# First weight tile of an attention and feed-forward kernel loaded later and converted in halves, second-pass inputs reordered, first products of the last stage moved forward

## The chip, the cores and the metric

The kernel runs on one core of a Trainium2 chip. Its time is the device time in microseconds (us) of one execution. A core has a matrix engine (TensorE, PE in the profile, its weight loads PEld), a vector engine (VectorE, DVE), a scalar engine (ScalarE, ACT), a general engine (GpSimd, POOL) and a queue that issues transfers (SyncE, SP). Each of them works through its own list of instructions in order and waits for the others by semaphores.

## What is computed

Eight batches of eight heads, 576 positions, head size 64: masked softmax attention, then for each of the 4608 tokens a feed-forward layer of 512 to 2048 to 512 with a sigmoid gate.

```python
scores = scale * np.matmul(q, k.transpose(0, 1, 3, 2))
# heads 0 to 3: 0 <= i - j < 32; heads 4 to 7: j <= i and i % 32 == j % 32
scores = np.where(masks[None], scores, -1e9)
attn = np.exp(scores - np.max(scores, axis=-1, keepdims=True))
attn = attn / (np.sum(attn, axis=-1, keepdims=True) + 1e-09)
x = np.matmul(attn, v).transpose(0, 2, 1, 3).reshape(B * S, H * D)
h = x @ w_in
g = h * (1.0 / (1.0 + np.exp(-1.702 * h)))
out = g @ w_out
```

## The kernel before

**Numbers.** Every matmul of the feed-forward layer is made of three, since each factor is held as a high and a low part: `x_high`, `w_high`, `t_high` round a tile to its high part on ACT, and `x_low`, `w_low_part`, `t_low` subtract that from the tile on DVE. A weight tile of w_in arrives as 64-bit words (1024 KB) and is turned into float32 in three steps, `w_scale` and `w_low` on ACT and `w_join` on DVE; `w_high` then makes the high part and stores the joined words to memory (`plains`) for later. The store stands behind the copy in program order, on SP.

**Stages.** The attention is cut into 48 pairs, six for each batch. A pair goes through `scores` (PE), `masked` (DVE), `exps` (ACT), `totals` (DVE), `scaled` (POOL), `turn` (four transposes on PE and a copy on ACT), `values` (PE) and its moves (copies on ACT, or on ACT and DVE when shared). The feed-forward layer's first half, per batch, follows its six pairs. For batch 0 (the first pass) it is done plainly: `plain(n, u)`, eight units of six matmuls for each of eight weight tiles n. From batch 1 on (the second pass and later) it is done by the seven products of a Strassen scheme, `product(n, k)` with `combine(n, k)`, on the sums of x parts (`x_sum`) and of weight parts (`t_sum` on POOL). The hidden values go to memory (`hid`). The second stage, `products(n)` for 72 pieces n, reads them back (`load_g`), applies the gate (`g_act`), makes sums on POOL (`g_sums`) and high and low parts (`g_split`), and multiplies them with w_out.

**Order.** All engines' orders are the order of the program. The pairs of batch 0 come first, written out by hand: a loop over pairs 0 to 4, then pair 5 and the rest of each pair's steps, with dummy matmuls (`fill`) between them. SP's first loads are pairs 0 to 5 and the first two weight tiles (`load_w(0)` behind `load_qk(3)`, `load_v(2)`). Then `plain(0, 0)`, and behind it on SP the loads of pairs 6 and 7 and of weight tile 2. From there on, a step counter s: at each s one unit or product of PE is written, and behind it what `side(s, f, ...)` has put there. `scores(6)` stands at s = 2, so behind `plain(0, 2)` on PE. The first pass has steps 0 to 60, and `HEAD` = 61 is the first product of the second pass; the last units of weight tile 7 lie between the first products (steps 62, 64, 66). `product(9, 1)` stands at step 70. `first(B) - 1` = 452 is the last step; the last three products, the first products of the second stage and their `g_split` are written out behind it.

**Units and weights.** Units 0 to 3 of weight tile 0 need quarters 0 and 3 of it (`HALVES`), and units 4 to 7 quarters 1 and 2. `plain(0, 2)` writes the bank that `values(5)` writes before.

Of the kernel before, what the change touches and what calls it, by code (L numbers as in the profile page):

```python
# [70 lines left out]
def attn_ffn(ctx, tc, qk, vs, weights, masks, ident, out):  # L71
# [326 lines left out]
    def w_words(which, i, raw):  # L398

        words[i] = raw[:, 2048:].bitcast(F32).rearrange("p (q n) -> p q n", q=4)  # L400
        view = raw[:, :2048].rearrange("p (q n w) -> p q n w", q=4, w=2)
        sync.dma_start(out=view, in_=weights[which][i])
        return view

    def w_scale(raw):
        f = raw[:, :, :, 1].bitcast(F32)
        scalar.activation(f, f, AF.Prelu, scale=2.0**-112, alpha=2.0**32)

    def w_low(raw):
        scalar.activation(  # L410
            raw[:, :, :, 0], raw.bitcast(U8)[:, :, :, 3], AF.Copy, scale=1 / 32, bias=-15.5 / 32
        )

    wv, words = {}, {}

    def w_join(i):
        raw = raws[i]
        vector.scalar_tensor_tensor(
            out=words[i].bitcast(U32), in0=raw[:, :, :, 1], scalar=3, in1=raw[:, :, :, 0],
            op0=ALU.logical_shift_left, op1=ALU.bitwise_or,  # L420
        )

    def w_high(i):
        wv[i] = w_tile(f"w_{i}").rearrange("p (k s n) -> p k s n", k=7, s=2)
        scalar.copy(out=wv[i][:, 0:4, 0], in_=words[i])
        sync.dma_start(out=plains[i].rearrange("p (q n) -> p q n", q=4), in_=words[i])

    def w_low_part(i):
        hi, lo = (wv[i][:, 0:4, s] for s in range(2))
        vector.tensor_tensor(out=lo, in0=words[i], in1=hi.bitcast(F32), op=ALU.subtract)  # L430

# [110 lines left out]
    for i in range(2, n0):  # L542
        load_qk(i)
        load_v(i - 1)
        if i == 3:
            load_w(0)
    load_v(n0 - 1)
    load_w(1)
    all_banks = [m_banks[i][x] for x in ("mx", "my", "mz") for i in range(2)]
# [5 lines left out]

    FILL = ((7, 0), (2, 0), (2, 3), (0, 1), (1, 0))
    for i in range(n0 - 1):
        late = all_banks[4 + i % 2]
        if i == 4:
            w_scale(raws[0])  # L560
        fill(FILL[i][0], late)
        ss = all_banks[2 * (i % 2) : 2 * (i % 2) + 2]
        scores(i, ss)
        if i >= 3:
            moves_of([values(i - 3, s_banks)])
        fill(FILL[i][1], late)
        if i >= 2:
            turn(i - 2, late)
        masked(i, ss)
        exps(i, ss)  # L570
        if i >= 1:
            totals(i - 1, ss)
            scaled(i - 1, ss)
    w_low(raws[0])
    scores(5, all_banks[2:4])
    masked(5, all_banks[2:4])
    exps(5, None)
    moves = values(2, s_banks)
    fill(1, all_banks[4])
    moves_of([moves])  # L580
    turn(3, all_banks[5])
    fill(1, all_banks[4])
    for i in (4, 5):
        totals(i, None)
        scaled(i, None)
    x_high(0, 0)
    w_join(0)
    x_low(0, 0)
    moves_of([values(3, s_banks, True)])
    x_high(3, 0)  # L590
    x_low(3, 0, gpsimd)
    fill(1, all_banks[5])
    turn(4, all_banks[4])
    fill(1, all_banks[5])
    w_high(0)
    w_low_part(0)
    turn(5, all_banks[5])
    moves_of([values(4, s_banks, True)])
    fill(2, all_banks[4])
    moves_of([values(5, all_banks[2:4], True)])  # L600
    plain(0, 0)
    for i in range(2):
        load_qk(n0 + i)
        load_v(n0 + i)
# [49 lines left out]
    for b in range(B):  # L654
        at = first(b)
        if b == 1:
            for t, f, k in ((-10, x_sum, 1), (-9, x_sum, 3), (-9, x_high, 4), (-8, x_low, 4),
                            (-7, x_sum, 2), (-6, x_high, 1), (-5, x_low, 1), (-3, x_high, 0),
                            (-2, x_low, 0), (-1, x_high, 2), (0, x_low, 2), (1, x_sum, 4),
                            (2, x_high, 3), (3, x_low, 3), (4, x_high, 6), (5, x_low, 6),  # L660
                            (6, x_high, 5), (7, x_low, 5)):
# [36 lines left out]
    for i in range(FP):  # L698
        load = -15 + i if i < 3 else 7 * i - 20
        sums, high, low = (-9, -4, -1) if not i else (7 * i - 10 + t + (i == 1) for t in (0, 6, 8))  # L700
        for m in range(4):
# [125 lines left out]

    def products(n):
        s, q = divmod(n, NB)
        banks = set_banks(s)  # L830
        for x, w, bank, part in PLACES:
            o = banks[bank][:, part * 256 : (part + 1) * 256]
# [40 lines left out]
    side(last - 5, load_g, 2)  # L873
    side(last + 28, load_g, 3)
    for i, n in enumerate((0, 1, 2, 3)):
        side(last + 15 + 8 * i, g_act, n)
        side(last + 16 + 8 * i, g_sums, n)
    for i in range(2):
        side(last + 24 + 3 * i, g_split, 0, slice(i, i + 1))

# [17 lines left out]
    for k in range(4, 7):  # L898
        product(B * FP - 1, k)
        combine(B * FP - 1, k)  # L900
        if k > 4:
            g_split(1, slice(k - 5, k - 4))
# [6 lines left out]
    for n in range(SETS * NB):  # L909
# [11 lines left out]
        if n % NB == 0 and n:  # L921
            finish(n // NB - 1)
        products(n)
    finish(SETS - 1)
# [99 lines left out]
```

## Time and profile before

| | |
|---|---|
| median of 3 runs | 847.76 us (845.82 to 848.14) |
| profiled execution | 846.93 us |
| its span, first to last instruction | 845.0 us |
| mean granted TensorE clock | 0.991 |
| busy: PE / PEld | 830.3 us (98%) / 807.1 us (96%) |
| busy: DVE / ACT / POOL | 539.1 / 421.7 / 476.5 us |

PE is busy nearly all the time, so the places count where it stands still or runs at a lower granted clock (0.50 in a row is 1.2 GHz, 1.00 is 2.4 GHz). A timeline row gives the start, the duration, the engine, and the operation with output and inputs, merged over neighbours of one kind; in brackets is how long the engine had been idle and what ended that.

### The profile page before, as it was taken

Reading aid. Unit: us, or ns where it says so; the run is one execution under the profiler, and the core shown is the slowest. Engines: PE = TensorE matmul, PEld = TensorE weight load, DVE = VectorE, ACT = ScalarE, POOL = GpSimd, SP = SyncE. Lnnn points to the kernel's source line nnn. Section 1 sums busy time; section 2 is a strip of 40 time slices with the busy share of each in tenths; the row PEclk is TensorE's granted clock in tenths of the full one; section 3 lists DMA queues with packets and bytes.
Section 4 is the critical chain, followed back from the end, with each engine's and each line's share of the span. In section 5 each row is a group of like instructions: output and inputs, shape, how many; then the busy total and the mean of one; then the engine's idle time right before and its main releaser. Section 6 shows DMA issues by size and latency. Waiting matters only on the chain. (4 is left out here: it accounts for less than half of the span.)

```text
span 845.0 us, 23947 instructions
## 1 busy us (share of the span) xinstructions
PE 830.3 (98%) x9820; PEld 807.1 (96%) x9826; DVE 539.1 (64%) x870; ACT 421.7 (50%) x664; POOL 476.5 (56%) x508
## 2 busy tenths in 40 slices
PE   7999999999999999999999999999999999999998
PEld 4899899999999999999999999999999999999998
DVE  5775776956777758577777765666545554555454
ACT  4775444434344434343446655555555555555550
POOL 2233877333442433234435269999877777777770
PEclk9899999999999999999999999999999999999999
DMA  8898676586785775866678954444444334433421
GB/s 334 308 392 287 195 243 199 169 251 219 218 265 180 239 230 187 259 215 211 225 250 254 273 168 135 141 135 162 129 131 144 126 125 133 143 126 125 135 91 51
DMA packets 112238, 164.84 MB, mean 195 GB/s; under 512 B 9728, under 2 KB 88320, under 8 KB 111104
## 3 DMA queue, kind: packets, MB, share of 16 engines
q1 hardware_dynamic: 112128, 163.31, 59.3%
q8 instruction: 77, 1.26, 0.6%
q14 instruction: 33, 0.27, 0.1%
HBM read 104.55 MB, written 58.72 MB: 193 GB/s over the span
## 5 line engine op out<-in xcount | busy, mean ns | idle before, releaser
L87 POOL TENSOR_TENSOR arena<-arena 128x256 f32<-128x256 f32 (+1 forms) x302 | 309.4, 1037 | 161.6 <-ACT arena L87 81.6
L87 DVE TENSOR_TENSOR xa<-arena,xa 128x576 fp32r<-128x576 f32 (+2 forms) x101 | 150.0, 1486 | 101.7 <-ACT xa L87 55.4
L87 PE MATMUL my<-xa,w 128*128 128x288 f32 x1140 | 181.2, 300 | 1.2 <-DVE arena L87 1.2
L87 ACT CAST xa<-arena 128x576 fp32r<-128x576 f32 (+2 forms) x102 | 115.2, 1148 | 104.9 <-PE s L87 76.1
L87 PEld LDWEIGHTS my<-xa,w 128*128 128x128 f32 x1140 | 159.0, 189 | 4.0 <-DVE arena L87 2.1
L87 ACT COPY arena<-mx 128x288 f32<-128x288 f32 (+4 forms) x181 | 62.8, 366 | 180.8 <-PE mx L87 138.5
L87 PE MATMUL mx<-xa,w 128*128 128x288 f32 x804 | 129.5, 299 | 1.7 <-ACT xa L87 1.2
L87 PE MATMUL mz<-xa,w 128*128 128x288 f32 x792 | 127.9, 299 | 0.0
L87 DVE TENSOR_TENSOR arena<-my,arena 128x288 f32<-128x288 f32 (+1 forms) x204 | 88.9, 442 | 53.6 <-PE my L87 51.9
L87 PEld LDWEIGHTS mx<-xa,w 128*128 128x128 f32 x804 | 114.0, 190 | 2.9 <-ACT xa L87 1.4
L87 ACT ACTIVATE arena<-arena 128x1024 f32<-128x1024 f32 (+2 forms) x120 | 105.2, 877 | 20.2 <-POOL arena L87 10.7
L87 PEld LDWEIGHTS mz<-xa,w 128*128 128x128 f32 x792 | 111.0, 189 | 1.4 <-DVE arena L87 0.3
L87 POOL TENSOR_TENSOR arena<-arena,nmax 128x432 f32<-128x432 f32 (+1 forms) x42 | 51.9, 1236 | 105.2 <-DVE nmax L87 95.4
L87 DVE TENSOR_TENSOR arena<-mz,arena 128x288 f32<-128x288 f32 (+1 forms) x166 | 70.0, 439 | 27.5 <-PE mz L87 19.0
L87 DVE TENSOR_TENSOR ga<-arena,ga 128x1792 fp32r<-128x1792 f32 (+1 forms) x25 | 51.9, 2077 | 52.9 <-ACT ga L87 35.9
L87 POOL TENSOR_TENSOR arena<-arena,rinv 96x512 f32<-96x512 f32 (+1 forms) x48 | 49.1, 1023 | 64.9 <-DVE rinv L87 51.2
L87 PE MATMUL mz<-w_out,xa 128*128 128x256 f32 x576 | 75.5, 280 | 0.0
L87 PE MATMUL mx<-w_out,xa 128*128 128x256 f32 x576 | 75.4, 280 | 0.0
L87 PE MATMUL my<-w_out,xa 128*128 128x256 f32 x576 | 75.3, 280 | 0.0
L87 PEld LDWEIGHTS mx<-w_out,xa 128*128 128x128 f32 x576 | 71.1, 188 | 0.0
L87 PEld LDWEIGHTS my<-w_out,xa 128*128 128x128 f32 x576 | 71.0, 188 | 0.0
L87 PEld LDWEIGHTS mz<-w_out,xa 128*128 128x128 f32 x576 | 70.9, 188 | 0.0
(75 smaller groups left out, 1017.9 us busy)
## 6 DMA issues: line engine op xcount, KB each, us to landing
hid<-arena SPq DMA_DIRECT2D x256, 144.0 KB, 3.3
arena<-hid SPq DMA_DIRECT2D x144, 256.0 KB, 3.2
arena<-qk SPq DMA_DIRECT2D x23, 448.0 KB, 4.9
arena<-qk SPq DMA_DIRECT2D x21, 472.0 KB, 5.7
arena<-vs SPq DMA_DIRECT2D x23, 384.0 KB, 4.7
out<-arena SPq DMA_DIRECT2D x34, 256.0 KB, 2.8
raw<-w_in SPq DMA_DIRECT2D x8, 1024.0 KB, 8.5
stage<-w_out SPq DMA_DIRECT2D x16, 512.0 KB, 4.2
```

The source lines that it names most:

```text
L87: ins = call(*args, **kw)
```

## The change

Four edits. (1) `load_w(0)` moves behind the last load of pair 5 and becomes two transfers: quarters 0 and 3, then 1 and 2 (`FIRST`). (2) The conversion of weight tile 0 is done in those halves: the scaling of the first half stands behind the moves of pair 2, and ahead of `exps(5)`; the second half's steps stand behind `x_high(3)`, and the store of the joined words, ahead of the loads of pairs 6 and 7 on SP, behind the second `w_high`. The dummy matmuls are dealt out anew (20 instead of 22). (3) In the second pass, `x_high(4)` and `x_low(4)` move from steps 52, 53 to 64, 65, `x_sum(2)`, `x_high(1)`, `x_low(1)` one step forward, `x_high(6)`, `x_low(6)` one back, and `t_high(0)` from step 57 to 59, which puts it behind `x_high(0)`. (4) At the end, the halves of `g_split(0)` move from steps 421 and 424 to 430 and 432, `load_g(3)` from 425 to 433, `g_act(3)` and `g_sums(3)` five steps back, and the first two of the seven places of `products(0)` move between the last three products of the first stage. No other arithmetic is added or left out.

```diff
--- before.py
+++ after.py
@@ -399,35 +399,42 @@
 
         words[i] = raw[:, 2048:].bitcast(F32).rearrange("p (q n) -> p q n", q=4)
         view = raw[:, :2048].rearrange("p (q n w) -> p q n w", q=4, w=2)
-        sync.dma_start(out=view, in_=weights[which][i])
+        for some in (ALL,) if i else FIRST:
+            sync.dma_start(out=view[:, some], in_=weights[which][i][:, some])
         return view
 
-    def w_scale(raw):
-        f = raw[:, :, :, 1].bitcast(F32)
+    ALL = slice(0, 4)
+    FIRST = slice(0, 4, 3), slice(1, 3)
+
+    def w_scale(raw, some=ALL):
+        f = raw[:, some, :, 1].bitcast(F32)
         scalar.activation(f, f, AF.Prelu, scale=2.0**-112, alpha=2.0**32)
 
-    def w_low(raw):
+    def w_low(raw, some=ALL):
         scalar.activation(
-            raw[:, :, :, 0], raw.bitcast(U8)[:, :, :, 3], AF.Copy, scale=1 / 32, bias=-15.5 / 32
+            raw[:, some, :, 0], raw[:, some].bitcast(U8)[:, :, :, 3], AF.Copy,
+            scale=1 / 32, bias=-15.5 / 32,
         )
 
     wv, words = {}, {}
 
-    def w_join(i):
-        raw = raws[i]
+    def w_join(i, some=ALL):
+        raw = raws[i][:, some]
         vector.scalar_tensor_tensor(
-            out=words[i].bitcast(U32), in0=raw[:, :, :, 1], scalar=3, in1=raw[:, :, :, 0],
-            op0=ALU.logical_shift_left, op1=ALU.bitwise_or,
+            out=words[i][:, some].bitcast(U32), in0=raw[:, :, :, 1], scalar=3,
+            in1=raw[:, :, :, 0], op0=ALU.logical_shift_left, op1=ALU.bitwise_or,
         )
 
-    def w_high(i):
-        wv[i] = w_tile(f"w_{i}").rearrange("p (k s n) -> p k s n", k=7, s=2)
-        scalar.copy(out=wv[i][:, 0:4, 0], in_=words[i])
-        sync.dma_start(out=plains[i].rearrange("p (q n) -> p q n", q=4), in_=words[i])
-
-    def w_low_part(i):
-        hi, lo = (wv[i][:, 0:4, s] for s in range(2))
-        vector.tensor_tensor(out=lo, in0=words[i], in1=hi.bitcast(F32), op=ALU.subtract)
+    def w_high(i, some=ALL):
+        if i not in wv:
+            wv[i] = w_tile(f"w_{i}").rearrange("p (k s n) -> p k s n", k=7, s=2)
+        scalar.copy(out=wv[i][:, 0:4, 0][:, some], in_=words[i][:, some])
+        if some != FIRST[0]:
+            sync.dma_start(out=plains[i].rearrange("p (q n) -> p q n", q=4), in_=words[i])
+
+    def w_low_part(i, some=ALL):
+        hi, lo = (wv[i][:, 0:4, s][:, some] for s in range(2))
+        vector.tensor_tensor(out=lo, in0=words[i][:, some], in1=hi.bitcast(F32), op=ALU.subtract)
 
     def t_view(k):
         if "sums" not in made:
@@ -542,9 +549,8 @@
     for i in range(2, n0):
         load_qk(i)
         load_v(i - 1)
-        if i == 3:
-            load_w(0)
     load_v(n0 - 1)
+    load_w(0)
     load_w(1)
     all_banks = [m_banks[i][x] for x in ("mx", "my", "mz") for i in range(2)]
 
@@ -553,11 +559,9 @@
         for _ in range(n):
             matmul(bank, lhsT=zeros[:, :P], rhs=zeros, start=True, stop=True)
 
-    FILL = ((7, 0), (2, 0), (2, 3), (0, 1), (1, 0))
+    FILL = ((7, 0), (2, 0), (2, 2), (0, 1), (0, 1))
     for i in range(n0 - 1):
         late = all_banks[4 + i % 2]
-        if i == 4:
-            w_scale(raws[0])
         fill(FILL[i][0], late)
         ss = all_banks[2 * (i % 2) : 2 * (i % 2) + 2]
         scores(i, ss)
@@ -571,34 +575,41 @@
         if i >= 1:
             totals(i - 1, ss)
             scaled(i - 1, ss)
-    w_low(raws[0])
     scores(5, all_banks[2:4])
     masked(5, all_banks[2:4])
+    moves_of([values(2, s_banks)])
+    w_scale(raws[0], FIRST[0])
     exps(5, None)
-    moves = values(2, s_banks)
     fill(1, all_banks[4])
-    moves_of([moves])
     turn(3, all_banks[5])
     fill(1, all_banks[4])
     for i in (4, 5):
         totals(i, None)
         scaled(i, None)
+    w_low(raws[0], FIRST[0])
     x_high(0, 0)
-    w_join(0)
+    w_join(0, FIRST[0])
     x_low(0, 0)
-    moves_of([values(3, s_banks, True)])
+    move = values(3, s_banks, True)
+    fill(1, all_banks[5])
+    turn(4, all_banks[4])
+    moves_of([move])
+    w_high(0, FIRST[0])
+    w_low_part(0, FIRST[0])
+    fill(1, all_banks[4])
+    turn(5, all_banks[5])
     x_high(3, 0)
     x_low(3, 0, gpsimd)
-    fill(1, all_banks[5])
-    turn(4, all_banks[4])
-    fill(1, all_banks[5])
-    w_high(0)
-    w_low_part(0)
-    turn(5, all_banks[5])
+    w_scale(raws[0], FIRST[1])
+    w_low(raws[0], FIRST[1])
+    w_join(0, FIRST[1])
     moves_of([values(4, s_banks, True)])
-    fill(2, all_banks[4])
-    moves_of([values(5, all_banks[2:4], True)])
+    fill(1, all_banks[4])
+    move = values(5, all_banks[2:4], True)
     plain(0, 0)
+    w_high(0, FIRST[1])
+    moves_of([move])
+    w_low_part(0, FIRST[1])
     for i in range(2):
         load_qk(n0 + i)
         load_v(n0 + i)
@@ -654,10 +665,10 @@
     for b in range(B):
         at = first(b)
         if b == 1:
-            for t, f, k in ((-10, x_sum, 1), (-9, x_sum, 3), (-9, x_high, 4), (-8, x_low, 4),
-                            (-7, x_sum, 2), (-6, x_high, 1), (-5, x_low, 1), (-3, x_high, 0),
-                            (-2, x_low, 0), (-1, x_high, 2), (0, x_low, 2), (1, x_sum, 4),
-                            (2, x_high, 3), (3, x_low, 3), (4, x_high, 6), (5, x_low, 6),
+            for t, f, k in ((-10, x_sum, 1), (-9, x_sum, 3), (-8, x_sum, 2), (-7, x_high, 1),
+                            (-6, x_low, 1), (-3, x_high, 0), (-2, x_low, 0), (-1, x_high, 2),
+                            (0, x_low, 2), (1, x_sum, 4), (2, x_high, 3), (3, x_low, 3),
+                            (3, x_high, 4), (4, x_low, 4), (5, x_high, 6), (6, x_low, 6),
                             (6, x_high, 5), (7, x_low, 5)):
                 side(at + t, f, k, b)
         elif b:
@@ -697,7 +708,7 @@
             side(at + t, f, i)
     for i in range(FP):
         load = -15 + i if i < 3 else 7 * i - 20
-        sums, high, low = (-9, -4, -1) if not i else (7 * i - 10 + t + (i == 1) for t in (0, 6, 8))
+        sums, high, low = (-9, -2, -1) if not i else (7 * i - 10 + t + (i == 1) for t in (0, 6, 8))
         for m in range(4):
             side(HEAD + sums, t_sum, i, m)
         for t, f in ((load, t_load), (high, t_high), (low, t_low)):
@@ -825,10 +836,10 @@
     def set_banks(s):
         return [m_banks[s % 2][x] for x in ("mx", "my", "mz")] + [s_banks[s % 2]]
 
-    def products(n):
+    def products(n, some=slice(0, 7)):
         s, q = divmod(n, NB)
         banks = set_banks(s)
-        for x, w, bank, part in PLACES:
+        for x, w, bank, part in PLACES[some]:
             o = banks[bank][:, part * 256 : (part + 1) * 256]
             for a in range(2):
                 fp = 2 * q + a
@@ -871,12 +882,13 @@
     side(last - 6, load_g, 0)
     side(last + 8, load_g, 1)
     side(last - 5, load_g, 2)
-    side(last + 28, load_g, 3)
-    for i, n in enumerate((0, 1, 2, 3)):
-        side(last + 15 + 8 * i, g_act, n)
-        side(last + 16 + 8 * i, g_sums, n)
+    side(last + 36, load_g, 3)
+    for n in range(4):
+        at = last + 15 + 8 * n + 5 * (n == 3)
+        side(at, g_act, n)
+        side(at + 1, g_sums, n)
     for i in range(2):
-        side(last + 24 + 3 * i, g_split, 0, slice(i, i + 1))
+        side(last + 33 + 2 * i, g_split, 0, slice(i, i + 1))
 
 
     units = {s: i for i, s in enumerate([*range(HEAD), HEAD + 1, HEAD + 3, HEAD + 5])}
@@ -898,6 +910,8 @@
     for k in range(4, 7):
         product(B * FP - 1, k)
         combine(B * FP - 1, k)
+        if k < 6:
+            products(0, slice(k - 4, k - 3))
         if k > 4:
             g_split(1, slice(k - 5, k - 4))
     for h in (12, 13):
@@ -920,7 +934,7 @@
         load_g(n + 6)
         if n % NB == 0 and n:
             finish(n // NB - 1)
-        products(n)
+        products(n, slice(0 if n else 2, 7))
     finish(SETS - 1)
```

## Rows read from the trace of the kernel before

**Rows 1.** Busy time in stretches of 20 us: the stretch, its length, then busy us (and instructions) of PE, PEld, DVE, ACT and POOL, the granted clock of TensorE, the share of the DMA engines and GB/s.

```profile
20.00:40.00 20.00, 19.20 (x312) 16.82 (x306) 14.83 (x27) 13.53 (x25) 5.08 (x4) 0.80 0.77 292
...
80.00:100.00 20.00, 18.15 (x189) 17.29 (x190) 11.82 (x17) 7.59 (x16) 12.33 (x13) 0.91 0.67 216
...
500.00:520.00 20.00, 20.00 (x171) 20.00 (x171) 12.90 (x12) 11.73 (x10) 19.29 (x18) 1.00 0.47 148
```

**Rows 2.** What PE waited for in the whole span: who waited and for whom, us in total, times, longest.

```profile
PE mx L87 <- DMA early<-qk: 2.7, 2, 1.8
...
PE mx L87 <- ACT xa L87: 1.2, 1, 1.2
```

**Rows 3.** Timeline of PE in the first 50 us: `scores(5)`, the first plain units (mx) and the third (my), `scores(6)`, and `turn(6)`.

```profile
18.93 1.12 PE L87 MATMUL my<-early 64*64 64x54 f32 x32 [0.71 <-DMA early<-qk]
...
29.28 1.86 PE L87 MATMUL mx<-xa,w 128*128 128x288 f32 x12
30.98 0.95 PE L87 MATMUL my<-xa,w 128*128 128x288 f32 x6
31.86 0.69 PE L87 MATMUL s<-arena 64*64 64x54 f32 x32
...
41.97 0.66 PE L87 MATMUL s<-ident_sb,arena 128*128 128x128 f32 x4 [0.35 <-POOL arena L87]
```

**Rows 4.** Busy time in chosen stretches, columns as in rows 1; two of them follow each other after the first 14 us, two lie where the first pass ends.

```profile
14.00:16.00 2.00, 0.28 (x3) 0.03 (x1) 0.20 (x2) 1.96 (x3) 1.04 (x1) 1.00 1.02 408
...
17.80:28.05 10.25, 8.91 (x163) 7.02 (x161) 7.24 (x16) 7.34 (x15) 5.08 (x4) 0.50 0.53 194
...
92.60:95.00 2.40, 0.65 (x3) 0.20 (x3) 0.99 (x2) 2.25 (x5) 2.16 (x4) 1.00 0.32 76
...
96.30:99.76 3.46, 3.46 (x17) 3.46 (x16) 2.94 (x6) 1.21 (x3) 2.51 (x2) 0.51 0.81 266
```

**Rows 5.** Transfers by issue, each from a window that holds this one alone: count, size, us from issue to landing. In order: q and k of pair 4 (issued at 6.48), of pair 5 (issued at 7.74), v of pair 5 (issued at 9.7), and q and k of pair 6.

```profile
early<-qk SPq DMA_DIRECT2D x1, 472.0 KB, 9.5
...
early<-qk SPq DMA_DIRECT2D x1, 472.0 KB, 11.1
...
early<-vs SPq DMA_DIRECT2D x1, 256.0 KB, 10.4
...
arena<-qk SPq DMA_DIRECT2D x1, 472.0 KB, 5.4
```

**Rows 6.** SP: its timeline around the first store of joined words, with the load of pair 6 behind it, and its longest wait from 10 to 30 us.

```profile
24.33 0.33 SPq L87 DMA_DIRECT2D plains<-raw  x1
24.76 0.38 SPq L87 DMA_DIRECT2D arena<-qk  x1
...
SPq L87 <- DVE raw L87: 11.9, 1, 11.9
```

**Rows 7.** Groups of instructions from 14 to 33 us, shapes kept apart: engine, operation, tiles, count, busy us, mean ns of one, then the idle time before them. In order: `x_high`, `w_low`, `w_scale`, the copy of `turn` for pairs 3 to 5, `exps`, `w_join`, `w_high`.

```profile
L87 ACT CAST xa<-arena 128x576 fp32r<-128x576 f32 x4 | 2.6, 677 | 0.0
...
L87 ACT ACTIVATE raw<-raw 128x1024 uint32<-128x1024 uint8 x2 | 2.3, 1136 | 0.0
L87 ACT ACTIVATE raw<-raw 128x1024 f32<-128x1024 f32 x2 | 2.3, 1134 | 0.0
...
L87 ACT COPY arena<-mz 128x512 f32<-128x512 f32 x3 | 1.8, 587 | 0.8 <-PE mz L87 0.8
...
L87 ACT ACTIVATE arena<-arena 128x432 f32<-128x432 f32 x3 | 1.7, 575 | 1.4 <-DVE arena L87 1.4
...
L87 DVE SCALAR_TENSOR_TENSOR raw<-raw 128x1024 uint32<-128x1024 uint32 x1 | 1.4, 1426 | 0.0
...
L87 ACT CAST w<-raw 128x1024 fp32r<-128x1024 f32 x1 | 1.0, 1048 | 0.0
```

**Rows 8.** Timeline of ACT: the copy of `turn(3)` and `x_high(0)`, one right behind the other.

```profile
22.77 0.58 ACT L87 COPY arena<-mz 128x512 f32<-128x512 f32 x1 [0.34 <-PE mz L87]
23.25 0.68 ACT L87 CAST xa<-arena 128x576 fp32r<-128x576 f32 x1
```

**Rows 9.** Timelines from 92 to 106 us, where the second pass begins. PE: the first matmul of `product(8, 0)`, and `product(9, 1)`. ACT: `t_high(0)`. DVE: `x_low(2)`, `x_low(3)`, `t_low(1)`. POOL: `below(12)`.

```profile
94.03 0.40 PE L87 MATMUL mx<-xa,w 128*128 128x288 f32 x1 [1.18 <-ACT xa L87]
...
104.88 1.29 PE L87 MATMUL my<-xa,w 128*128 128x288 f32 x6
...
92.06 1.05 ACT L87 CAST w<-sums 128x1024 fp32r<-128x1024 f32 x1 [1.95 <-POOL sums L87]
...
96.54 1.47 DVE L87 TENSOR_TENSOR xa<-arena,xa 128x576 fp32r<-128x576 f32 x1
...
99.62 0.71 DVE L87 TENSOR_TENSOR xa<-arena,xa 128x576 fp32r<-128x576 f32 x1
...
104.11 1.21 DVE L87 TENSOR_TENSOR w<-sums,w 128x1024 fp32r<-128x1024 f32 x1
...
95.60 1.79 POOL L87 TENSOR_TENSOR arena<-arena,nmax 128x432 f32<-128x432 f32 x1
```

**Rows 10.** Timelines near the end of the first stage. PE: `product(60, 3)`, and `product(63, 5)`, the last but one. DVE: the low part of a half tile of w_out, with the adds of products queued behind it.

```profile
462.60 1.06 PE L87 MATMUL my<-xa,w 128*128 128x288 f32 x6 [0.49 <-DVE arena L87]
...
482.05 1.06 PE L87 MATMUL my<-xa,w 128*128 128x288 f32 x6 [0.75 <-DVE arena L87]
...
460.92 1.26 DVE L87 TENSOR_TENSOR w_out<-arena,w_out 128x896 fp32r<-128x896 f32 x1
```

## The prediction

> **What bounds the kernel now.** I read the busy time by stretches first, then what PE waited for, then the timelines of the few places where it stood still. PE is the bound: from the second stage on, a stretch of 20 us holds 20.00 us of PE work [rows 1]. So work taken off another engine is worth nothing by itself, and only two things count: time in which PE stands still, and time at the lower granted clock. Both are in the first 40 us and where the second pass begins: the stretch 20 to 40 has a granted clock of 0.80, 80 to 100 has 18.15 us of PE work at 0.91 [rows 1]. The waits say why: 2.7 us and 0.71 us for pairs that had not landed [rows 2, 3], 1.18 us for `x_high(0)` of the second pass [rows 2, 9], 0.49 and 0.75 us for DVE near the end of the first stage [rows 10]. The clock follows the standstills: PE had 0.28 us of work between 14 and 16, and then ran from 17.8 to 28.05 at 0.50; it had 0.65 us of work between 92.6 and 95, and ran from 96.3 to 99.76 at 0.51 [rows 4]. All later work hangs on PE, so what one place gains or loses reaches the end nearly whole.
>
> **Part 1, the loads.** The last transfer that stands 5,336 KB into SP's list is pair 5's q and k now; it lands at 7.74 + 11.1 = 18.84 [rows 5]. Pair 4's, 4,608 KB in, lands at 6.48 + 9.5 = 15.98. With the 1,024 KB of weights behind them, pair 4 stands at 3,584 KB and pair 5 at 4,312. Read off between those two landings and earlier ones at the same rate, some 380 KB per us, they land at about 13.3 and 15.2. So both waits for pairs, 2.5 us, go. The first weight half takes the place at 5,336 KB: it lands at about **18.8**, and ACT, which by my reckoning is ready for it at 18.3, waits for it.
>
> **Part 2, the conversion.** From there I follow ACT, since it now does everything in one line: first `w_scale`, `exps(5)`, the copy of `turn(3)`, first `w_low`, `x_high(0)`, the copy of `turn(4)`, moves of pair 3, first `w_high`, the copy of `turn(5)`, `x_high(3)`, second `w_scale`, second `w_low`; then DVE does the second `w_join`. Widths are in rows 7: a half of `w_scale` or `w_low` is 512 wide; half of 1.13 us would be 0.57, the 512-wide copy is 0.59, and I take 0.62, four times; `w_high` 0.57; `exps` 0.57; three copies of 0.59; two `x_high` of 0.68; the moves, two short copies, 0.5 by estimate. That is 2.48 + 0.57 + 0.57 + 1.76 + 1.36 + 0.5 = 7.2 us. Neighbours overlap by 0.1 (0.58 us from 22.77, and the next begins at 23.25 [rows 8]), which takes off 1.2: 6.0 us. `turn(4)` is not ready when ACT is, as it needs the copy of `turn(3)` and `values(3)` on PE first: 0.4 us at the full clock, 1.2 at half; I take 0.7. The join takes half of 1.43 [rows 7], 0.7. So the words are whole at 18.8 + 6.0 + 0.7 + 0.7, about **26.3**; they are whole at 24.3 now. If the weights came before ACT asked for them it would be 25.2; if ACT waited for both halves, as the last transfers ahead of them land at 9.7 + 10.4 = 20.1 [rows 5], 27.6.
>
> PE's side of it gets earlier: with no wait for pairs and little of the lower clock, `plain(0, 0)` needs only the first half. On the same line of ACT the first `w_high` ends at about 23.4 and the copy of `turn(5)` at 23.9; `values(4)` and `values(5)` behind that, some 0.7 us of PE past the copy, make it about 24.7 instead of 29.28 [rows 3]. If that were all, 4.6 us would be won.
>
> **What is late next.** The store of the joined words stands on SP ahead of the load of pair 6. SP stood 11.9 us for the join, issued the store at 24.33 and pair 6 at 24.76, which landed 5.4 us later, at 30.16 [rows 5, 6]: 5.85 us behind the join. PE reaches `scores(6)` at 31.86 now, without a wait [rows 3]. With the words whole at 26.3, pair 6 lands at 26.3 + 5.85, about **32.2**, while PE has done its first three units by 27.6 or, held by the moves of pair 5 behind the second `w_high`, 28.2. PE can take nothing behind `scores(6)`, so it stands for about 4 us and goes on 0.3 us later than now (between 31.05 and 33.4: 0.8 us earlier to 1.6 later). Behind a standstill half as long the clock fell [rows 4]. The stretch at half clock costs half of itself: 1.7 us if it is 3.46 us long, 5.1 if it is 10.25. What follows here is dense, as behind 96.3, so I take 4.4 us, a cost of **2.2**; at the least 0. The next slack, PE's 0.35 us before `turn(6)` [rows 3], gives back nothing I can count. Part 1 and 2 together: +0.3 + 2.2 = **+2.5 us** (from -0.8 to +6). The two dummy matmuls left out cost nothing where PE waits anyway.
>
> By the Trainium skill (DMA: Bandwidth & Descriptors, section Anatomy of one DMA — SWDGE (gpsimd) path), a transfer costs some 2.0 us and its bytes at 436 GB/s, a fit for another issue path. For the store and pair 6, 1.0 MB, an estimate by that page is 4.3 us where the rows have 5.85; by it part 1 and 2 would come to +1.0, and I stay with the rows.
>
> **Part 3, the second pass.** `t_high(0)` waited 1.95 us for POOL's sums [rows 9] and held up two copies and `x_high(0)` behind it on ACT, and `product(8, 0)` waited for that. Moved behind `x_high(0)`, it holds up nothing that PE needs at once: `x_high(0)` runs from about 90.9, behind the copy of `plain(7, 2)`, `x_low(0)` ends at about 92.8, and PE goes on there rather than at 95.0. The standstill, 1.75 us of the 2.4 from 92.6 on, and the 1.7 us that the half clock costs go [rows 4]: 3.5 us at most. But `x_low(4)`, 1 us, comes into DVE's queue between `x_low(3)` and `x_low(6)`, and `t_low(1)` stands behind all of it. `product(9, 1)` waits for `t_low(1)` already (it starts at 104.88, takes 1.29 us, and `t_low(1)` ends at 105.3 [rows 9]). `x_low(3)` waits in DVE's order for the totals of pair 12, so for `below(12)`, which POOL, full from 86 on, ends at 97.4 [rows 9]; that is not moved. From 97.9 I count on DVE: totals 0.9, `x_low(3)` 0.7, `x_low(4)` 1.0, mask and maxima of pair 13 1.5, an add 0.4, `x_low(6)` 0.9, `t_low(1)` 1.2, less overlaps, to 104.1. So 1.2 of the 3.5 us arrive: **-1.2 us**, from -3.5 to +0.5 (PE's new wait of 1.5 us there could bring a half-clock stretch back).
>
> The Trainium skill (GPSIMD Engine Reference, section Key points) says that POOL shares its ports to the on-chip memory with DVE instructions of two inputs from it. The rows agree: 1.47 us for `x_low(2)` beside a busy POOL, 0.71 for `x_low(3)` beside an idle one [rows 9].
>
> **Part 4, the end.** The 0.75 us before `product(63, 5)` is filled by six matmuls that are ready: -0.7. The 0.49 us before `product(60, 3)` [rows 10] comes from the backlog of DVE, 1.26 us of w_out and two 1.1 us halves of `g_split(0)` ahead of the adds; moved nine steps on, these stand ahead of the add for `product(61, 3)`, so I count -0.2 of it. SP's load behind the second half waits as before. **-0.9 us** (-1.25 to +0.3).
>
> **Sum.** +2.5 - 1.2 - 0.9 = +0.4 us on the profiled execution's 846.93 (span 845.0): 847.3. That execution lies 0.83 under the median of the runs, 847.76, and I forecast against the median: **848.2 us**.
>
> **Rivals.** (a) *All of it arrives.* Pair 6 is no limit and the clock holds: -4.6 at the start, -3.5 and -1.25 later, 838.4. For it speaks that every wait named is truly taken away; against it, that the words would have to be whole at 21.5, with 6 us of ACT's work behind 18.8. Chance 0.06. (b) *Half of it.* Words early (25.2) and no half clock behind the standstill: -0.8, then -2.2 and -1.1: 843.7. For it: low clock needs a cause in the trace each time, and PE's standstill might be shorter. Chance 0.16. (c) *Slower by the clock.* The half-clock stretch behind `scores(6)` is the long one of rows 4: +0.3 + 5.1 - 1.2 - 0.9 = +3.3, 851.1. It decides from a stretch of 8.4 us on. For it: the long one also followed waits for pairs; against it: that stretch had 1.3 us of gaps, and here plain units follow in a dense row. Chance 0.20. (d) *DVE gives nothing back.* The four differences ahead of `t_low(1)` all run beside a busy POOL, at the longer of the two prices in rows 9: four times 0.76 us, less 0.7 already counted, is +2.3, so part 3 comes to about +1.1 and the time to 850.5, on the edge. It decides where POOL has no pause left between 97 and 104. The Trainium skill's page on GpSimd, above, names its cause. Chance 0.08, half of it slower.
>
> **Chances.** My forecast, with a spread of 2 us either side, has 0.50. A measurement here can tell about 0.3% from no change, 2.5 us. Faster: (a), (b) and a little of the forecast's edge, 0.24. Slower: (c), half of (d), 0.24. Within: 0.52. The range leaves out (a) and the far ends: from (b) to a little beyond (c), 843.4 to 852.0; the forecast's own is 846.2 to 850.2.
>
> **What would show it.** First the wait of PE ahead of `scores(6)`: about 4 us for the load of pair 6, at 28 to 32, with the store issued at about 26.3 and a granted clock of 0.5 for some us behind it; no waits for pairs 4 and 5; `plain(0, 0)` near 24.7. Then no wait of PE at the first product of the second pass, the clock at 1.00 there, and instead a wait near `product(9, 1)` for `t_low(1)`. At the end, no wait before `product(63, 5)`. I am wrong if pair 6 lands before 29, if the clock stays up through the standstill, or if PE gains over 2.5 us between 85 and 110.

## The result, and the profile after

| | before | after |
|---|---|---|
| median of 6 runs each | 847.1 us (845.82 to 848.14) | 853.62 us (851.69 to 855.63) |
| ratio to before, 95% interval | | 1.0077 (1.0061 to 1.0093) |
| profiled execution (its span) | 846.93 (845.0) | 853.34 (851.4) |
| mean granted TensorE clock | 0.991 | 0.993 |

The change costs 6.5 us. I had forecast 848.2 us, most likely no measurable change, in 843.4 to 852.0: the time lies above the range.

I read the same places as before. First PE's timeline in the first 50 us, against [rows 3]: `turn(0)`, the second piece of `values(0)`, `scores(5)` in two pieces, the plain units, `scores(6)`, `turn(6)`.

```profile
11.57 0.55 PE L87 MATMUL mz<-ident_sb,arena 96*128 96x96 f32 x4 [1.54 <-POOL arena L87]
...
13.63 0.82 PE L87 MATMUL s<-arena 64*64 64x32 f32 x27 [0.38 <-issue]
...
18.69 0.33 PE L87 MATMUL my<-early 64*64 64x54 f32 x7
20.09 0.61 PE L87 MATMUL my<-early 64*64 64x54 f32 x25 [1.06 <-issue]
...
28.08 1.86 PE L87 MATMUL mx<-xa,w 128*128 128x288 f32 x12
30.77 1.07 PE L87 MATMUL my<-xa,w 128*128 128x288 f32 x6 [0.83 <-ACT arena L87]
34.78 1.12 PE L87 MATMUL s<-arena 64*64 64x54 f32 x32 [2.94 <-DMA arena<-qk]
...
46.43 0.66 PE L87 MATMUL s<-ident_sb,arena 128*128 128x128 f32 x4 [0.64 <-POOL arena L87]
```

The waits for pairs 4 and 5 (2.7 us in [rows 2]) are gone. In their place stands 2.94 us for pair 6, and `scores(6)` is 2.92 us later than before, `turn(6)` 4.46. In `scores(5)` there is a standstill of 1.06 us that the profile gives to "issue": PE waited for nothing that the profile shows. The experiments come back to it.

SP's timeline (the store, and the load of pair 6 behind it), against [rows 6]:

```profile
29.82 0.33 SPq L87 DMA_DIRECT2D plains<-raw  x1
30.25 0.38 SPq L87 DMA_DIRECT2D arena<-qk  x1
```

SP's longest wait from 10 to 32 us, and the landing of pair 6's load, issued in the window 30 to 31:

```profile
SPq L87 <- DVE arena L87: 16.7, 1, 16.7
```

```profile
arena<-qk SPq DMA_DIRECT2D x1, 472.0 KB, 4.5
```

SP stood 16.7 us for the second join (11.9 before); pair 6 lands at 30.25 + 4.5 = 34.75, and `scores(6)` starts at 34.78. ACT's timeline says why the words come so late, against [rows 8]: the moves of pair 2, the first `w_scale`, the second `w_scale` and `w_low` together, the second `w_high`.

```profile
21.41 0.54 ACT L87 COPY arena<-s 128x192 f32<-128x192 f32 x2 [1.79 <-PE s L87]
21.84 0.68 ACT L87 ACTIVATE raw<-raw 128x512 f32<-128x512 f32 x1
...
27.64 1.24 ACT L87 ACTIVATE raw<-raw 128x512 f32<-128x512 f32 x2
...
29.83 0.62 ACT L87 CAST w<-raw 128x512 fp32r<-128x512 f32 x1 [0.70 <-DVE raw L87]
```

ACT comes to the first half at 21.84, not for want of weights (issued at 8.91, landed 9.0 us later, at 17.9) but because it waited 1.79 us for PE. Busy time in chosen stretches, columns as in rows 1, shows the clock: at the start, behind `scores(6)`, and in the second pass.

```profile
14.00:17.60 3.60, 3.27 (x93) 2.99 (x88) 1.53 (x5) 1.49 (x4) 1.04 (x1) 0.53 1.02 356
...
34.78:37.20 2.42, 2.42 (x38) 2.32 (x38) 1.31 (x2) 1.04 (x1) 0.00 (x0) 0.50 1.07 398
...
109.80:112.50 2.70, 2.70 (x39) 2.32 (x39) 0.78 (x2) 1.02 (x5) 2.27 (x3) 0.50 0.53 164
```

The second pass, against [rows 9]: first PE (`product(8, 3)`, `product(9, 1)`), then DVE (`x_low(3)` with `x_low(4)`, then `t_low(1)`).

```profile
104.01 0.93 PE L87 MATMUL my<-xa,w 128*128 128x288 f32 x5 [0.55 <-DVE xa L87]
...
109.14 1.03 PE L87 MATMUL my<-xa,w 128*128 128x288 f32 x4 [1.90 <-DVE w L87]
```

```profile
103.25 2.09 DVE L87 TENSOR_TENSOR xa<-arena,xa 128x576 fp32r<-128x576 f32 x2
...
107.87 1.22 DVE L87 TENSOR_TENSOR w<-sums,w 128x1024 fp32r<-128x1024 f32 x1
```

The wait for `x_high(0)` is gone: from `scores(12)` to `product(9, 0)` PE gains 2.6 us. Then it waits 1.90 us for `t_low(1)`, at half clock behind it, and from `scores(12)` to `turn(13)` the pass is 0.75 us longer than before. The end, against [rows 10], PE's rows with a wait from 460 to 492 us:

```profile
471.12 1.07 PE L87 MATMUL my<-xa,w 128*128 128x288 f32 x6 [0.47 <-DVE arena L87]
...
473.47 1.06 PE L87 MATMUL mz<-xa,w 128*128 128x288 f32 x6 [0.50 <-DVE arena L87]
...
474.84 1.06 PE L87 MATMUL my<-xa,w 128*128 128x288 f32 x6 [0.30 <-DVE arena L87]
...
484.38 1.07 PE L87 MATMUL my<-xa,w 128*128 128x288 f32 x6 [0.55 <-DVE arena L87]
```

Both waits of [rows 10] are gone, the 0.75 us before `product(63, 5)` and the 0.49 before `product(60, 3)`. In their place stand the four above, before `product(60, 5)`, `product(60, 6)`, `product(61, 3)` and `product(62, 5)`: 1.82 us for 1.24.

### The profile page after: what moved, and what is told of

It reads as the page before. It is cut to its first block, busy times and chain, and to the rows that moved or that the text cites. A ratio compares the mean times of both kernels' runs of the same rounds, so it can differ in the third digit from the quotient of the medians.

```text
span 851.4 us, 23948 instructions
## 1 busy us (share of the span) xinstructions
PE 829.6 (97%) x9817; PEld 807.1 (95%) x9824; DVE 541.0 (64%) x872; ACT 421.7 (50%) x667; POOL 477.2 (56%) x508
```

## The experiments

Each kernel ran in five rounds beside the kernel before, whose median in the four sets was 846.94, 846.58, 847.05 and 847.3 us. I give each ratio to that with its 95% interval.

**One edit at a time**, each as its hunks in the diff above and nothing else. Edits 1 and 2 are the start, and go together first.

> The kernel before with the first two edits alone (later weight load, conversion in halves, new order at the start); second pass and end as before. Theory: the store of joined words stands ahead of pair 6's load on SP, so PE waits 2 to 4 us at scores(6) and runs some us at 1.2 GHz behind it; turn(6) comes about 4.5 us later than before, and the time rises by 3.5 to 5 us. Rival 1, that the loss of the whole change sits in the second pass and the end and the start is even: a rise under 1 us. Rival 2, that the wait for pair 6 was one execution's accident: no wait over 1 us at scores(6).

Measured 851.77 us, 1.0065 (1.0044 to 1.0085). `scores(6)` waits 2.78 us for pair 6, behind a store issued at 29.31.

> The kernel before with the third edit alone (order of the x parts and of t_high(0) in the second pass). Theory: the first products stand no longer, PE is 2 to 3 us ahead at product(9, 0), and gives that back at product(9, 1), where it waits 1.5 to 2 us for t_low(1) on DVE, with a half-clock stretch behind it: the time rises by 0.5 to 1.5 us. Rival: the wait at product(9, 1) came only from the late start of the whole, and alone the edit gains 2 us or more.

Measured 846.62 us, 0.9999 (0.9987 to 1.0011): even, neither the rise that I expected nor the rival's gain. PE's row at `product(9, 1)`:

```profile
102.47 0.81 PE L87 MATMUL my<-xa,w 128*128 128x288 f32 x4 [1.90 <-DVE w L87]
```

> The kernel before with the fourth edit alone (halves of g_split(0) later, two places of products(0) between the last products). Theory: 0.75 us before product(63, 5) is won, and 1.2 us is lost in three or four waits for DVE around the moved halves: between -0.3 and +0.7 us. Rival: the moved halves are harmless, and the waits in the changed kernel came from a shifted DMA rhythm: a gain of 0.8 to 1.3 us.

Measured 847.56 us, 1.0012 (1.0001 to 1.0024). The three parts add up: +0.65%, -0.01% and +0.12% make +0.76%, and the whole is +0.77%. PE's waits near the end in its trace, before `product(60, 6)`, `product(61, 3)` and `product(62, 5)`; the one before `product(60, 3)` is gone:

```profile
467.13 1.05 PE L87 MATMUL mz<-xa,w 128*128 128x288 f32 x6 [0.50 <-DVE arena L87]
...
468.49 1.06 PE L87 MATMUL my<-xa,w 128*128 128x288 f32 x6 [0.31 <-DVE arena L87]
...
477.98 1.06 PE L87 MATMUL my<-xa,w 128*128 128x288 f32 x6 [0.49 <-DVE arena L87]
```

DVE's timeline, with the two moved halves of `g_split(0)`:

```profile
462.77 1.58 DVE L87 TENSOR_TENSOR ga<-arena,ga 128x896 fp32r<-128x896 f32 x1 [0.42 <-ACT ga L87]
464.27 0.45 DVE L87 TENSOR_TENSOR arena<-my,arena 128x288 f32<-128x288 f32 x1
465.56 1.15 DVE L87 TENSOR_TENSOR ga<-arena,ga 128x896 fp32r<-128x896 f32 x1 [0.85 <-ACT ga L87]
466.63 0.44 DVE L87 TENSOR_TENSOR arena<-mz,arena 128x288 f32<-128x288 f32 x1
```

Each half makes DVE stand for ACT's half (0.42 and 0.85 us; before, 0.70 for the first alone) and takes 1.15 to 1.58 us, with the adds that PE needs queued behind.

**The store behind the loads.** The whole change, with the store of the joined words issued behind the loads of pairs 6 and 7 and of weight tile 2:

```diff
-        if some != FIRST[0]:
+        if some == ALL:
             sync.dma_start(out=plains[i].rearrange("p (q n) -> p q n", q=4), in_=words[i])
...
     load_w(2)
+    sync.dma_start(out=plains[0].rearrange("p (q n) -> p q n", q=4), in_=words[0])
```

> The changed kernel with one statement moved: the first store of joined words is issued behind the loads of pairs 6 and 7 and of weight tile 2. Theory: these loads go out at 11 to 13 us and have landed when PE asks, the wait of 2.9 us at scores(6) goes and with it most of the half-clock stretch behind it: 3.5 to 5 us faster than the changed kernel, some 849 us. Rival 1: the wait is only replaced by one for the conversion of the next weight tile or for ACT, and under 1.5 us is won. Rival 2: the half clock comes anyway, 2.5 to 3 us are won.

Measured 848.88 us, 1.002 (1.0008 to 1.0032): 4.7 us less than the whole change. PE's timeline:

```profile
29.34 1.06 PE L87 MATMUL my<-xa,w 128*128 128x288 f32 x6 [0.79 <-ACT arena L87]
30.33 0.69 PE L87 MATMUL s<-arena 64*64 64x54 f32 x32
...
41.38 0.66 PE L87 MATMUL s<-ident_sb,arena 128*128 128x128 f32 x4 [0.36 <-POOL arena L87]
```

`scores(6)` waits for nothing, pair 6 having been issued at 14.53. So the store's place is worth 4.7 of the 6.5 us. (The run of this trace took 847.12 us, so the kernel's other runs lose more than it shows.) The same cure on the start alone:

> Edits 1 and 2 alone, with the store of the joined words issued behind the loads of pairs 6 and 7 and of weight tile 2. Theory: the whole loss of the start is pair 6 standing behind the store, and with it gone the start gains a little: scores(6) has no wait for its pair, turn(6) comes near 41.4 as in the whole change with the same cure (41.97 before), and the time is 846.0 to 847.0. Rival: the conversion in halves costs by itself, since the kernel with all edits and this cure was still 0.2% over before, while edits 3 and 4 alone come to about 0.1%: then 847.5 to 848.5.

Measured 848.17 us, 1.0016 (1.0005 to 1.0028). The rival was right: with pair 6 out of the way the start still gains nothing, though PE waits less for pairs than before.

**Is it the later load?** Edits 1 and 2, with the two half transfers at the place that the load has before the change:

```diff
         load_v(i - 1)
+        if i == 3:
+            load_w(0)
     load_v(n0 - 1)
-    load_w(0)
     load_w(1)
```

> The first two edits alone, but with weight tile 0 loaded where the kernel before loads it (behind pair 3's q and k, in the same two transfers); conversion in halves as in the changed kernel. In start_only the first half had landed at 18 us, and ACT came to it only at 21 to 22. Theory, that the words are late because all of the conversion now stands in ACT's line behind the moves of pair 2, whatever the load does: the words are whole no earlier than in start_only (29.3), the waits for pairs 4 and 5 come back, and the time is 3.5 to 7 us over the kernel before. Rival, that the late load is the cause: the words are whole near 26, and the rise is under 2 us.

Measured 853.9 us, 1.0086 (1.0073 to 1.0099). With the weights loaded early, ACT comes to them at 22.07 and the store goes at 30.05, so the words are late even so. The run does not show that the late load costs nothing: with the early one, PE waits 2.47 us for pair 4 again, which holds up ACT too. In `scores(5)` it has no standstill. Nor is it a step of ACT alone: the first half's `w_scale` and `w_low` moved ahead of the moves of pair 2, into ACT's gap of 1.79 us:

```diff
-    moves_of([values(2, s_banks)])
     w_scale(raws[0], FIRST[0])
+    w_low(raws[0], FIRST[0])
+    moves_of([values(2, s_banks)])
     exps(5, None)
...
-    w_low(raws[0], FIRST[0])
     x_high(0, 0)
```

> The whole change, with the scaling and the low part of the first weight half put ahead of the moves of pair 2 on ACT, where ACT stood 1.79 us for PE with the weights already there. Theory: the words are late because the conversion stands in ACT's line; 1.2 us of the 8.0 us line go into that gap, so the store is issued at 28.6 to 29.0 (29.82 now), scores(6) starts at 33.4 to 33.9 (34.78 now), and the time falls by about 1 us, to 852.0 to 853.0. Rival: ACT's line isn't what decides, since it waits for PE at turn(4) and for DVE's join; then the store stays at 29.8 and the time at 853.6.

Measured 853.11 us, 1.0068 (1.0053 to 1.0084). My theory fell: the store went at 30.32. ACT waited for PE at other steps then, and PE had stood in `scores(5)` once more:

```profile
18.67 0.99 PE L87 MATMUL my<-early 64*64 64x54 f32 x25 [2.08 <-issue]
```

**The standstill in `scores(5)`.** It is in all five traces so far in which the load comes late, always behind the 7th matmul: 1.06 us in after, 1.07, 1.30, 2.08 and 3.21 (this last in the start with the late store). To see whether it hangs on the place in PE's list, 3 dummy matmuls ahead of the first pair instead of 7, on the kernel with the start and the late store:

```diff
-    FILL = ((7, 0), (2, 0), (2, 2), (0, 1), (0, 1))
+    FILL = ((3, 0), (2, 0), (2, 2), (0, 1), (0, 1))
```

> As the kernel with edits 1 and 2 and the store behind the loads, with 3 dummy matmuls instead of 7 ahead of the first pair, so that PE's list is 4 instructions shorter at that point. PE stood 1.06 to 1.30 us in scores(5) behind the 7th matmul in every kernel with edit 1. If the stop hangs on the place in PE's list, it comes now behind the 11th matmul (or behind as many as 4 matmul instructions make); if it hangs on the time or on what the queues carry, it comes behind another count or not at all. Time: within 1 us of the kernel with 7, by either.

Measured 849.5 us, 1.0034 (1.0021 to 1.0046), 1.3 us over the kernel with 7, a little more than the 1 us that I allowed. PE's timeline:

```profile
17.65 0.43 PE L87 MATMUL my<-early 64*64 64x54 f32 x11
20.56 0.79 PE L87 MATMUL my<-early 64*64 64x54 f32 x19 [2.48 <-issue]
```

Behind the 11th instead of the 7th: it is a place in the list. The shorter standstill ahead of it moves too, in `values(0)` from behind the 21st matmul to behind the 25th. From the one place to the other, the timeline of after counts 27 + 4 + 2 + 32 + 48 + 4 + 2 + 7 = 126 matmuls; with two dummies that the program has between, 128, each with its weight load: 256 instructions. Over the whole span of the kernel before, one DMA queue carries instructions in packets of this size,

```profile
q8 instruction: 77, 1.26, 0.6%
```

and its profile counts 9,820 instructions of PE and 9,826 of PEld: 255 to each of the 77 packets, so this queue is PE's. Between the two standstills it carries one packet of 0.02 MB; of after in the window 17.6 to 18.0, and of this kernel in 18.2 to 18.6 (packets, MB, share):

```profile
q8 instruction: 1, 0.02, 15.0%
```

```profile
q8 instruction: 1, 0.02, 15.4%
```

PE goes on at 20.09 and 20.56, about 2.2 us behind each packet. In ten traces that show the standstill, those of the next runs and one of 0.18 us in second_only included, the distance is 2.2 to 2.6 us, with packets anywhere from 14.7 to 18.3. The Trainium skill (Runtime: NRT & Kernel Launch, section Instruction fetch mechanics) has instructions come in blocks of 16 KiB, 256 at a time, by a queue of the engine's own, mostly hidden. The count of 256 and the packet of 0.02 MB agree with it; that the crossing is hidden does not hold in the traces above, with 1.06 to 3.21 us of standstill.

**Is the block late because of the loads?** The same start, with the loads of weight tiles 0 and 1, 2 MB, held back behind the mask of pair 3 by a write of one column:

```diff
-    load_w(0)
-    load_w(1)
...
         masked(i, ss)
+        if i == 3:
+            raws[0] = raw_tile("raw_0")
+            vector.memset(raws[0][:, 0:1], 0)
+            raws[0] = w_words(0, 0, raws[0])
+            load_w(1)
         exps(i, ss)
```

> Edits 1 and 2 with the store behind the loads, and the loads of weight tiles 0 and 1 held back, by a one-column write of DVE behind the mask of pair 3, from 9.5 us to about 14. Theory: PE's standstill in scores(5) is the wait for a 16 KB block of its own instructions, whose packet stands behind the loads in the queues; with 2 MB less in them the packet comes before 16 (16.3 to 18.4 so far) and PE goes on before 18.3, with a standstill under 1 us; the weights land at 18.5 to 20, still in time for ACT, and the time is 846.0 to 847.2. Rival: the packet comes a fixed time behind the block before it, whatever the loads; then the standstill is 1 to 3 us as before and the time 848 or more.

Measured 845.71 us, 0.9988 (0.9977 to 0.9999), against 1.0016 without the hold. The packet, in the window 14.6 to 15.0, then PE in `scores(5)`, then the stretch 12 to 40 (columns as in rows 1); behind them `scores(5)` and a stretch of the same kernel without the hold (start_store_late):

```profile
q8 instruction: 1, 0.02, 16.7%
```

```profile
15.93 0.33 PE L87 MATMUL my<-early 64*64 64x54 f32 x7
17.31 0.61 PE L87 MATMUL my<-early 64*64 64x54 f32 x25 [1.05 <-issue]
```

```profile
12.00:40.00 28.00, 23.08 (x485) 19.64 (x477) 20.95 (x47) 20.43 (x42) 8.31 (x8) 1.00 0.95 346
```

```profile
16.00 0.33 PE L87 MATMUL my<-early 64*64 64x54 f32 x7
19.54 0.61 PE L87 MATMUL my<-early 64*64 64x54 f32 x25 [3.21 <-issue]
```

```profile
20.98:34.75 13.77, 12.02 (x130) 9.84 (x130) 8.72 (x19) 10.80 (x24) 3.79 (x3) 0.50 0.68 252
```

Up to the place PE is as far in both (`scores(5)` starts at 15.93 and 16.00), and the DMA engines are busy all the time (360 GB/s from 12 to 20 with the hold, 405 without); but 2 MB less is queued early. The packet comes at 14.7 instead of 17.2, PE goes on at 17.31 instead of 19.54 (a standstill of 1.05 us, not under 1 as I expected), the clock stays at 1.00, and `turn(6)` starts at 40.03 (44.27 without the hold, 41.97 before). The run of the trace without the hold took 849.76 us, over its kernel's median of 848.17, so the two traces lie further apart than the medians do, 2.4 us. The whole change with the same hold, the store left where the change has it:

> The whole change with the same hold, the store where the change has it. Theory: the words still come out of ACT's line at 28.5 to 30, pair 6 behind them, so most of the loss stays: 852.0 to 853.5; the instruction wait in scores(5) gets shorter. Rival: the instruction wait was what made ACT late, and the words are whole near 27: 849 to 851.

Measured 850.32 us, 1.0035 (1.0021 to 1.0048): 3.3 us less than the whole change, the rival's number but not its reason: in `scores(5)` PE no longer stands (packet at 14.8), yet the store goes at 29.35 and `scores(6)` waits 1.98 us for pair 6. In this profile PE ran at a granted clock of 0.60 from 12 to 20, so the words came hardly earlier in it; its run took 852.28 us, and the gain over the runs is larger than this one trace explains.

**The two halves of the rest.** In the kernel before, `t_high(0)` put behind `x_high(0)` and nothing else:

```diff
-        sums, high, low = (-9, -4, -1) if not i else ...
+        sums, high, low = (-9, -2, -1) if not i else ...
```

> The kernel before with one number changed: t_high(0) two steps later, behind x_high(0) on ACT; x_high(4) and x_low(4) stay at their early place. Theory, that the third edit's gain at the first products is given back because x_low(4) was put ahead of t_low(1) on DVE: no wait at product(8, 0), a wait of about 1 us instead of 1.9 at product(9, 1), PE 1.5 to 2 us ahead by turn(13), the time 1 to 2 us lower. Rival, that POOL (below(12), at about 94 to 95 by second_only's clock) sets t_low(1) whatever stands ahead of it: the wait at product(9, 1) stays at 1.8 or more and the time is even.

Measured 847.49 us, 1.0007 (0.9998 to 1.0015). `product(9, 1)` waits 0.39 us instead of 1.90, and from `scores(12)` to `turn(13)` the trace is 1.3 us shorter than before; the runs don't show it. Of edit 4 only the last two hunks of the diff and `products` with `some`, that is the two places of `products(0)` between the last products, with `g_split(0)`, `load_g(3)`, `g_act(3)` and `g_sums(3)` where they were:

> The kernel before with two places of products(0) between the last products, and nothing else of the fourth edit. Theory, that the moved halves of g_split(0) cost what the places win: the wait of 0.75 us before product(63, 5) is filled, no new waits around 465 to 478, the time 0.5 to 0.9 us lower. Rival, that the two places only shift the wait to the next product or to the start of the second stage: even.

Measured 846.3 us, 0.9995 (0.9987 to 1.0004), no wait before `product(63, 5)` and no new one. Both together:

> The kernel before with t_high(0) two steps later and the two places of products(0) between the last products. Theory: the two gains add up, 1.5 to 3 us under the kernel before. Rival: one of them is eaten, under 1 us.

Measured 846.07 us, 0.9991 (0.9981 to 1.0001): under 1 us, as the rival had it, and not clear of no change.

**A version that beats both.** Start with the late store and the first half scaled early, `t_high(0)` and the two places; without and with the hold of the loads:

> Edits 1 and 2 with the store behind the loads and the first half's scaling ahead of the moves of pair 2; of edit 3 only t_high(0) behind x_high(0), of edit 4 only the two places of products(0) between the last first-stage products. Theory: each of these was even or slightly ahead by itself, so together 844.5 to 846.0, ahead of before by 0.6 to 2 us. Rival: what PE gains by a shorter start is given back where it next stands still, and the time is 846.5 as before.

Measured 848.19 us, 1.0008 (0.9996 to 1.002), with 2.47 us of standstill in `scores(5)`: not the gain that I expected, but even with the kernel before, as the rival had it.

> The same hold in the kernel with all the cures (store behind the loads, first half scaled ahead of the moves of pair 2, t_high(0) behind x_high(0), the two places of products(0) between the last first-stage products). Theory: without the wait for instructions the start is ahead of before, 844.5 to 846.0. Rival: the standstill stays, 848.

Measured 845.36 us, 0.9981 (0.997 to 0.9993), with 0.69 us of it. That is 8 us less than the change as made, and about 1.6 less than before. The hold does most of it: weights_held, without the other cures, was at 845.71.

## Why the prediction was wrong

- **What held.** The mechanism that I put first: the store stands on SP ahead of pair 6, the words come later than now, PE stands at `scores(6)` (2.94 us; I had said about 4) with a half-clock stretch behind (2.42 us at 0.50, a cost of 1.2; I had taken 2.2). Moving that store alone gives back 4.7 us. Pairs 4 and 5 landed at 13.4 and 15.3 (13.3 and 15.2; yet the two landings that I named are 254 KB per us apart, not 380). ACT's and DVE's line from the first `w_scale` to the join took 8.0 us (7.4 by my terms).
- **The step that failed first** is "ACT, which by my reckoning is ready for it at 18.3, waits for it". ACT came at 21.84 and waited for nothing of the weights, which had landed at 17.9. What hangs on ACT is late by the same 3.5 us, the words at 29.8 instead of 26.3; `plain(0, 0)` came at 28.08 instead of 24.7, and pair 6, 4.95 us behind the join and not 5.85, at 34.75 instead of 32.2. Part 1 and 2, forecast at +2.5, measured 0.65%, **+5.5 us**.
- **Why it failed**: I wrote that "both waits for pairs, 2.5 us, go", and let PE run on. Without them PE would have come to `scores(5)` at 16.44 instead of 18.93 [rows 3]; in after it came at 18.69, 2.25 us later than that, and stood there for 1.06 more: 3.3 of the 3.5. The standstill is the block of instructions that PE enters within `scores(5)`: its packet came at 17.9, and PE went on at 20.09. Before, the packet came at 16.2; with 2.2 to 2.6 us behind it the block was there by 18.8, and the wait for pair 5, up to 18.93, covered its coming. PE can be early here and gain nothing: in the seven traces with the late load and no hold it came to `scores(5)` at 16.0 to 18.7 and went on behind the place at 18.7 to 20.6. With the loads held the packet comes earlier, the standstill shrinks or goes, and the time falls by 2.4 us with the late store and by 3.3 in the whole change. Of the 2.25 us, 0.82 are there at `turn(0)` (11.57, against the row of before below), and in the 1.43 behind it lies the half clock from 14 to 17.6. These are figures of one trace: after_store_late, with the same order on PE, came to `scores(5)` at 17.03. Why the 2.25 us came, and how much of it other runs have, stays open.

```profile
10.75 0.55 PE L87 MATMUL mz<-ident_sb,arena 96*128 96x96 f32 x4 [0.38 <-POOL arena L87]
```

- **Part 3**, forecast -1.2, measured **0.0** (0.9999). The wait at `product(9, 1)` came as I said (1.90 for my 1.5). Its half-clock stretch, which I left to the bound of +0.5, was there in the trace with this edit alone (0.50 from 104 to 106) and in after (2.70 us, 1.35 lost), and took more than the rest: in both traces the pass is 0.8 us longer up to `turn(13)`. The cause that I named, `x_low(4)` in DVE's queue ahead of `t_low(1)`, agrees with t_high_only, which leaves it where it was: the wait is 0.39, and from `x_low(3)` to `t_low(1)` DVE takes 3.1 us instead of 4.6. That the time did not fall there either stays open. One reading was wrong: `x_low(3)` of before did not run beside an idle POOL, which worked from 99.85 on (the row below), and the subtraction at 105.25 took 0.75 us beside a POOL that was busy throughout. So the longer price of [rows 9], on which rival (d) counted, does not come with every busy POOL.

```profile
99.85 1.25 POOL L87 TENSOR_TENSOR arena<-arena,rinv 128x432 f32<-128x432 f32 x1 [0.34 <-DVE rinv L87]
```

- **Part 4**, forecast -0.9, measured **+1.0** (1.0012, so 0.1 to 2.0 us). Both waits went, 1.24 us. The step that failed is that the halves of `g_split(0)`, moved on, would still save 0.2 of the 0.49, so hold up 0.3 at their new place: they hold up 1.30 there (0.50, 0.31 and 0.49 us). By the trace that comes out even, and the +1.0 of the runs is not in these waits; where it lies stays open. The two places alone, without that move, are at 0.9995, and the two kernels were not measured beside each other.
- **The sum**: misses of +3.0, +1.2 and +1.9 us, all to one side, make 6.1 where +0.4 was forecast and +6.5 measured. Rival (c) had the direction and half the size (+3.3), but the wrong reason: the half clock behind `scores(6)` was shorter than I took, not longer.

## What to carry to other kernels

A transfer that waits for a computation, put ahead of loads on the same queue, is as late as the slowest step of that computation: issue what waits behind what doesn't, here 4.7 us. When a wait for data is taken from an engine, ask what else was arriving under its cover; instructions arrive by DMA as the loads do, later here when more loads were queued (packet at 17.2 against 14.7), so filling the queues early can cost the engine the time that the early data gave. Of an instruction that is moved, look what it will itself wait for at the new place, since everything behind it on its engine waits too.

## What I had not expected of the hardware

PE's own instructions are a transfer among the others. In five traces the packet came 3.6 to 4.2 us behind PE's first matmul past the place in `values(0)`, with the loads under way, and PE went on 2.2 to 2.6 us behind the packet, whatever its time. With 2 MB of loads held back to 13.2 to 14.7 us the packet came at 14.7 to 15.7 instead of 16.2 to 18.3. A profile names such a standstill "issue" and gives no releaser; that it moves from the 7th to the 11th matmul with four dummy matmuls less ahead is what gave it away. Whether the block's distance to its packet can be shortened, no run here shows.
